# A linear-attention layer feeding a Mish expert: decaying three states with a diagonal matrix on TensorE, one step's row sums on VectorE, and a new order of instructions

## The chip, the cores and the metric

The kernel runs on one core of a Trainium2 chip. The metric is the device time of one execution in microseconds (us); the kernel before is given by the median of three runs, 466.11 us (465.73 to 466.19). The engines are TensorE (PE in the profile, with its weight loads as PEld), VectorE (DVE), ScalarE (ACT), GpSimd (POOL) and SyncE (SP), which issues most of the DMA transfers.

## The reference

Two stages, batch 4, 8 heads, 768 positions, head size 48; then 3072 tokens, model size 384, hidden size 2048, all float32.

```python
for t in range(S):                                   # recurrent attention, per head
    cur = einsum('bhd,bhe->bhde', u * k[t], v[t])
    y[t] = einsum('bhd,bhde->bhe', r[t], state + cur)
    state = w[:, :, None] * state + einsum('bhd,bhe->bhde', k[t], v[t])
x = y as (tokens, heads * head_dim)
h = x @ w_in
g = h * tanh(softplus(h))
return g @ w_out
```

## The kernel before

**Attention.** The positions are cut into chunks of 64. A "step" s is one of 24 pieces of work: one chunk of two of the four batches, all heads; four steps (one "group" of 512 tokens, 128 positions of every batch) make the input of one pass of the second stage. A step loads `rk` (r and k, transposed), `rkn` or `kn` (k, and r where needed, by position) and `v`. VectorE scales `rk` by powers of the decay (`scale`, L640). TensorE makes scores (`scores`, L725), which VectorE copies under a mask into a matrix `P` whose diagonal holds row sums of u times r times k (`attend`, L746; `diag`, L694). The row sums are made in one of three ways (`dots`, L648): steps below `N_SQ` with a TensorE product into `yt`, steps below `N_PE` with 16 one-column float32 products into `pa` (in `scores`), later steps with three VectorE operations on `rkn` (L686 to L691), which need r in the load and the table `un`. Then TensorE makes the outputs (`rows_y`, L799, for steps from 2; `spread_y`, L772, for steps 0 and 1) from the state carried so far and from `P`, and the products for the new state (`state_products`, L957). Two steps can be under way at once: each of the two sets of states is updated every second step (`update_state`, L932): VectorE multiplies the state by the decay over 64 positions and adds the products from two PSUM banks (L947, L952). The function has another branch, for steps in `decayed(s)`: there TensorE has added diag(decay) times the state to the same PSUM sums (`decays`, L837), and the state is only copied out. With `N_DEC = 2` no step takes it. A table for k, the "token table" (L345), is made with TensorE once, from the matrices `dw` that hold the decay on a diagonal.

**Second stage.** Six groups of 512 tokens, each with 16 tiles of hidden columns. An "up" tile is a product of x and the first weight matrix into one of two `hp` banks; it is evacuated to `hb` (L1312), goes through a sigmoid, an arctangent and a sine on ScalarE (L1094 to L1100) and products on VectorE (L1110 to L1118), and a "down" tile adds its product with the second matrix to three `acc` banks. Group 0 uses plain float32 products for most tiles; the others split each factor in a high and a low part and use three products. Weight blocks (`raw`, 768 KB each) are converted from an integer form on ScalarE and VectorE (`convert`, L492, the last operation at L514) and split (`split`, L519).

**Order.** Every engine's instructions are emitted by a planner (`Flow`, L134): a list scheduler with modelled durations. Each piece of work is a generator that yields events to wait for and costs on engines; among those that are ready the earliest goes, ties by rank, and `SHIFT`, `RANK`, `CONVERT`, `LAG` and the like move ranks. The order of the first loads is the list `FIRST`, of those behind it `REST`. `LO0` to `HI1` say over which part of a group's 16 up tiles the next group's four steps are spread (`place`, L1033). `AHEAD_LEAST` and `AHEAD_MOST` bound the distance between up and down tiles.

**Idle products.** At the start TensorE runs products of zeros into the bank `idle`: ten 512-column ones first, then some ahead of the first pieces of work (`warm`, L389), as the table `WARM` says; some wait for a load or a conversion. At `dots0` 14 short ones (16 columns) stand in addition, at `attend0` 28 short ones stand in place of two full ones.

Of the kernel before, what the change touches and what calls it, by code (L numbers as in the profile page):

```python
# [61 lines left out]
    return q // 2, 2 * (q % 2) + j  # L62


N_DEC = 2
N_SQ, N_PE = 2, 6
OWN = 3
CHECK_AT, CHECK_STEP = 44, 3
DIAG_ACT = (0, 1, 2, 5, 6, 10)
AHEAD = 4  # L70
UNITS = [(h, c) for h in range(2) for c in range(AHEAD)] + [(None, f) for f in range(WG * AHEAD, NF)]

# [5 lines left out]
def first_use(c):  # L78
# [1 line left out]


FIRST = (
    ("rk", 0), ("rk", 1), ("raw", 0), ("rkn", 3), ("v", 0), ("rkn", 1), ("rk", 2), ("rkn", 2), ("raw", 1), ("v", 1),
    ("rkn", 0), ("v", 3), ("v", 2), ("rk", 3),
)
REST = (
    ("raw", 2), ("raw", 3), ("un", 0), ("raw", 4), ("rk", 4), ("v", 4), ("raw", 5), ("raw", 6), ("rkn", 4), ("raw",
    8), ("raw", 7), ("raw", 9), ("raw", 10), ("raw", 14), ("raw", 11), ("raw", 12), ("raw", 13), ("raw", 15),
)
LAND0, LAND = 3.15, dict(rk=1.32, v=0.66, raw=1.96, rkn=0.5, un=0.78)  # L90
# [3 lines left out]
PAIRS = ()  # L94
BY_STEP = 0
FROM, FROM2 = 8, 14
X_SPLIT = 2
CONVERT = (1848.944, -4805.376, -1293.02, -2635.977)
LAG = 6
AHEAD_LEAST, AHEAD_MOST, DOWN = 3, 8, 0  # L100
LO0, HI0, LO1, HI1 = 0.0, 0.8, 0.05, 0.65
LAT, LAT0 = 0.15, 0.13
PE_GAP = 33
DVE_OWN = 0.02
COLD, COLD_END = 1.0, 0.0
WARM0, WARM_MIN, FILL = 10, 0.3, 0.28
WARM_END = 14.0
SHORT, LEFT_OUT = dict(dots0=14, attend0=28), ("attend0",)
WARM = dict(
    dots0=(("rk0", 2),), attend0=((None, 2),), dots1=((None, 1),), attend1=((None, 4),),  # L110
    outputs1=((None, 2), ("bent0", 3), ("whole0", 2), ("masked1", 4)),
# [2 lines left out]
BLOCK0, BLOCK, ASK, HELD, FETCH = 445, 256, 0.7, 2.9, 2.5  # L114
PATIENCE = dict(dve=0.1, act=0.1, pe=0.3)
URGENT = 8
RANK = dict(token_table=-1938.0, keys=833.2, first_state=-421.9)

COST = dict(dve=1.0)
FREE = dict(pe=5.6, act=2.8, dve=1.0, pool=1.7, sp=1.0, landed=1.0)  # L120
# [2 lines left out]


SHIFT = dict(
    attend10=98.0, attend5=51.0, convert11=-5.0, convert6=32.0, convert7=-243.0, convert9=122.0, diag10=-20.0,
    diag6=24.0, dots10=19.0, dots5=30.0, dots7=-71.0, dots8=121.0, evacuate10=-99.0, evacuate13=-164.0,
    evacuate22=-66.0, finish2=31.0, finish9=-62.0, gate10=141.0, gate12=-83.0, gate2=-42.0, gate3=54.0, gate8=-83.0,
    keys11=-152.0, keys5=24.0, mix0=-2.0, mix18=-54.0, mix5=-59.0, mix8=-31.0, mix9=-95.0, outputs9=-134.0,
    scale5=-174.0, split14=-67.0, split3=2.3, split4=73.0,  # L130
)


# [113 lines left out]
class Us(float):  # L247
    n = 0
# [17 lines left out]
def rwkv_mish_kernel(ctx, tc, rkT, rkN, vN, wT, w_in, w_out, consts, rkF, vF, wF, uF, outT):  # L266
    nc = tc.nc
# [9 lines left out]
    un = const.tile([128, DM], F32, name="un")  # L277
# [89 lines left out]
    def matmul(out, lhsT, rhs, **flags):  # L367
        nonlocal count
        ins = nc.tensor.matmul(out, lhsT=lhsT, rhs=rhs, **flags)  # L369
        first, count = count, count + (4 if lhsT.dtype == F32 else 2)  # L370
        k = (count - 1 - BLOCK0 % BLOCK) // BLOCK
        if k != (first - 1 - BLOCK0 % BLOCK) // BLOCK:
            crossed[k] = ins
        return ins
# [14 lines left out]
    def warm(name):  # L389

        z = zeros.bitcast(BF16)[:, :1]
        for after, n in WARM.get(name, ()):
            flow.begun += 2 * n
            for k in range(0 if name in LEFT_OUT else n):
                ins = matmul(idle, lhsT=z.broadcast_to([128, 128]), rhs=z.broadcast_to([128, 512]), start=True, stop=True)
                if after in marks and not k:
                    tc.add_manual_dep(ins.ins, marks[after].ins.name, sync, reason="no idle product goes too soon")
        for _ in range(SHORT.get(name, 0)):
            nc.tensor.matmul(
                idle[:32, :16], lhsT=z.broadcast_to([128, 32]), rhs=z.broadcast_to([128, 16]), start=True, stop=True  # L400
            )

    pa = ps.tile([128, 2, 512], F32, name="pa", tag="pa")
    for i in range(2):
# [5 lines left out]
    idle = ps.tile([128, 512], F32, name="idle", tag="acc0")  # L410
# [283 lines left out]
    def diag(s):  # L694
        yield f"sd{s}"
        if s >= 2:
            yield f"out{s - 2}"
        engine = yield {"act": 1.15} if s in DIAG_ACT else {"dve": 0.68}
        sd = sums.pop(s)
# [96 lines left out]
    def decayed(s):  # L796
        return 2 <= s < min(N_DEC, NS - 2)

# [82 lines left out]
    def outputs(s):  # L881
# [33 lines left out]
        if not rows:  # L915
            flow.start(first_state(s), s + RANK["first_state"], name=f"first_state{s}")
        elif not last:
# [548 lines left out]
    for s in range(NS):  # L1466
        if s < 2:
            flow.start(spread_v(s), rank(s) + 0.0045, 0.0, f"spread_v{s}")
        for k, thread in enumerate((load_step, load_v, scale, dots, diag, keys, attend, outputs)):
            if thread is keys and s >= NS - 2 or s <= B and thread in (load_step, load_v):  # L1470
                continue
            if thread is keys and s < B:
                flow.start(keys(s), s + (RANK["keys"] if s < 2 else -899.8), 0.0, f"keys{s}")
                continue
# [4 lines left out]
    for h in range(2) if FROM < WG * AHEAD else (None,):  # L1479
        flow.start(split_x(h), X_SPLIT, 0.0, f"split_x{'' if h is None else h}")  # L1480
    flow.start(load_rest(), -1200, 0.0)
    flow.start(prologue(), -1100, 0.0, "prologue")
    flow.start(token_table(), RANK["token_table"], 0.0, "token_table")
    for c in range(len(W_ORDER)):
        i, f = W_ORDER[c]
        at = first_use(f) + (LAG - L_OUT if i else -L_IN) + c / 1000
        flow.start(convert(c), CONVERT[c] if c < len(CONVERT) else at, 0.0, f"convert{c}")
    for n, (i, f) in enumerate(S_ORDER):
        first = first_use(f) if split_early((i, f)) else NF + f * WG
        flow.start(split(n), first + (LAG - L_OUT if i else -L_IN) + n / 1000, 0.0, f"split{n}")  # L1490
    flow.start(ups(), 1000, 0.0)
# [10 lines left out]
    with tc.If(in_range < 128 * N_FLAGS):  # L1502
# [3 lines left out]
        with tc.tile_pool(name="any1", bufs=1) as work:  # L1506
# [4 lines left out]
            z = work.tile([128, N, D], F32, name="z")  # L1511
# [39 lines left out]
        with tc.tile_pool(name="any2", bufs=1) as work:  # L1551
# [15 lines left out]
            z = zeros.bitcast(BF16)[:, :1]  # L1567
# [123 lines left out]
```

## Time and profile before

| | us |
|---|---|
| median of three runs | 466.11 |
| lowest, highest | 465.73, 466.19 |
| the profiled execution | 465.52 |
| its span, first to last instruction | 463.7 |
| TensorE busy | 454.9 (98%) |
| VectorE busy | 368.9 (80%) |
| ScalarE busy | 398.4 (86%) |
| mean granted TensorE clock | 0.990 |

Times within the profile count from the first instruction. Busy times are unions over an engine's instructions; a product that TensorE runs is drawn with its start and a modelled end, and products overlap, so the step from one start to the next tells more than a product's length. A float32 product is recorded as two.

### The profile page before, as it was taken

The numbers are of one execution on the slowest core, as the hardware profiler recorded it, in microseconds if no ns is written. First come the engines' busy times: TensorE is split into PE (matmuls) and PEld (weight loads), VectorE is DVE, ScalarE is ACT, GpSimd is POOL, SyncE is SP. The second block draws the span as 40 slices with busy tenths as digits, with TensorE's granted clock in tenths as the row PEclk, the third lists the DMA queues.
The fourth block names the chain that finished last, engine by engine and source line by source line (L and its number), as shares of the span: only waits on it lengthen the run. The fifth ranks groups of instructions, "written<-read, shape, count | busy, mean of one in ns | idle before, by whom it ended". The sixth has DMA issues, their size and how long they took to land.

```text
span 463.7 us, 11622 instructions
## 1 busy us (share of the span) xinstructions
PE 454.9 (98%) x4966; PEld 385.4 (83%) x4966; DVE 368.9 (80%) x584; ACT 398.4 (86%) x515; POOL 4.4 (1%) x31
## 2 busy tenths in 40 slices
PE   8999999999999999999999999999999999999995
PEld 5688988756887888888888888888888888888884
DVE  6899999999799995699956789974898746646752
ACT  5678989999899897787899888899888899999981
POOL 1000000000000000000000000000000000000000
PEclk8899999999999999999999999999999999999999
DMA  8866765730422230334241545432353222142001
GB/s 294 324 221 212 278 220 174 259 107 1 166 87 84 69 103 9 121 131 144 90 154 54 191 158 201 157 112 69 146 174 109 75 80 69 68 136 70 1 1 72
DMA packets 20169, 60.16 MB, mean 130 GB/s; under 512 B 3312, under 2 KB 4304, under 8 KB 20112
## 3 DMA queue, kind: packets, MB, share of 16 engines
q1 hardware_dynamic: 17664, 55.11, 34.9%
q10 hardware_dynamic: 2448, 4.25, 2.4%
q8 instruction: 40, 0.66, 0.6%
q14 instruction: 17, 0.14, 0.1%
HBM read 52.57 MB, written 4.72 MB: 124 GB/s over the span
## 4 chain that ended last, share of the span: by engine, by line
PE 74%; ACT 11%; DVE 10%; issue 2%; DMA 1%; ACTq 1%; SPq 0%; DVEq 0%
PE hp L369 33%; PE acc L369 32%; PE pa L369 4%; DVE hb L1110 2%; PE yt L369 2%; ACT fa L1100 2%; ACT L1094 2%; ACT fa L1094 2%; ACT fa L1097 2%; ACT L1100 1%; PE idle L369 1%; DVE gl L1118 1%; DMA rk<-in_rkT_dram 1%; DVE w L532 1%; ACT we L451 1%
## 5 line engine op out<-in xcount | busy, mean ns | idle before, releaser
L369 PE MATMUL hp<-x,w 128*128 128x512 f32 x720 | 169.0, 381 | 0.9 <-DVE hb L1312 0.9
L369 PE MATMUL acc<-gh,w 128*128 128x512 f32 x492 | 158.2, 381 | 0.0
L369 PEld LDWEIGHTS hp<-x,w 128*128 128x128 f32 x720 | 135.2, 189 | 20.8 <-DVE hb L1312 1.1
L369 PEld LDWEIGHTS acc<-gh,w 128*128 128x128 f32 x492 | 93.0, 189 | 13.5
L369 PE MATMUL acc<-gl,w 128*128 128x512 f32 x246 | 92.6, 379 | 0.0
L1110 DVE TENSOR_TENSOR hb<-hb,fa 128x1024 f32<-128x1024 f32 x40 | 48.9, 1221 | 36.8 <-ACT fa L1100 36.6
L1094 ACT ACT_TABLE_LOAD x47 | 60.3, 1283 | 5.7 <-DVE hb L1110 4.6
L1100 ACT ACT_TABLE_LOAD x47 | 60.3, 1283 | 1.7 <-DVE rkn L686 0.9
L1094 ACT ACTIVATE fa<-hb,small 128x1024 f32<-128x1024 f32 x48 | 55.2, 1151 | 2.1 <-DVE hb L1110 1.5
L369 PEld LDWEIGHTS acc<-gl,w 128*128 128x128 f32 x246 | 46.5, 189 | 6.6
L1097 ACT ACTIVATE fa<-fa 128x1024 f32<-128x1024 f32 x48 | 50.7, 1057 | 1.1 <-ACT fa L1094 0.3
L1312 DVE COPY hb<-hp 128x512 f32<-128x512 f32 x48 | 32.7, 685 | 23.2 <-PE hp L369 22.9
L1100 ACT ACTIVATE fa<-fa 128x1024 f32<-128x1024 f32 x47 | 49.7, 1058 | 0.5
L1118 DVE TENSOR_TENSOR gl<-hb,gh 128x1024 fp32r<-128x1024 f32 x40 | 48.8, 1219 | 1.0 <-ACT gh L1114 0.4
L1312 ACT COPY hb<-hp 128x512 f32<-128x512 f32 x48 | 28.0, 583 | 18.8 <-PE hp L369 18.7
L369 PE MATMUL acc<-gf,wraw 128*128 128x256 f32 (+1 forms) x132 | 37.8, 439 | 0.8 <-PE hp L369 0.8
L369 PEld LDWEIGHTS acc<-gf,wraw 128*128 128x128 f32 x132 | 25.8, 196 | 10.6 <-issue 7.0
L640 DVE TENSOR_TENSOR rk<-rk,TR 112x1024 f32<-112x1024 f32 x22 | 26.7, 1216 | 0.1
L1114 DVE CAST gh<-hb 128x1024 fp32r<-128x1024 f32 x32 | 22.0, 687 | 1.1
L369 PE MATMUL hp<-x,wraw 128*128 128x256 f32 x96 | 22.5, 386 | 0.0
L369 PEld LDWEIGHTS hp<-x,wraw 128*128 128x128 f32 x96 | 18.4, 196 | 2.0
L451 ACT ACTIVATE we<-wraw 128x768 f32<-128x768 f32 x16 | 19.3, 1207 | 0.7 <-ACT we L1152 0.4
(150 smaller groups left out, 554.6 us busy)
## 6 DMA issues: line engine op xcount, KB each, us to landing
wraw<-in_w_in_dram SPq DMA_DIRECT2D x16, 768.0 KB, 4.2
wraw<-in_w_out_dram SPq DMA_DIRECT2D x16, 768.0 KB, 4.9
rk<-in_rkT_dram SPq DMA_DIRECT2D x22, 512.0 KB, 4.4
rkn<-in_rkN_dram SPq DMA_DIRECT2D x18, 384.0 KB, 4.5
v<-in_vN_dram SPq DMA_DIRECT2D x22, 256.0 KB, 4.6
out_dram<-ob ACTq DMA_DIRECT2D x10, 256.0 KB, 2.1
x<-x SPq DMA_DIRECT2D x60, 32.0 KB, 2.0
out_dram<-we ACTq DMA_DIRECT2D x6, 256.0 KB, 2.2
```

The lines of the kernel that those rows point to most:

```text
L369: ins = nc.tensor.matmul(out, lhsT=lhsT, rhs=rhs, **flags)
L451: nc.scalar.activation(e, raw[:, :, 1].bitcast(F32), AF.Square, accum_out=to[:, 1:2])
L532: nc.vector.tensor_tensor(out=w[:, 1], in0=e, in1=w[:, 0].bitcast(F32), op=ALU.subtract)
L640: nc.vector.tensor_tensor(out=ab, in0=ab, in1=TR[:112].unsqueeze(1).broadcast_to([112, 4, NP, CK]), op=ALU.mult)
L1094: nc.scalar.activation(o.g, o.hb, AF.Sigmoid, bias=bias_ln2, scale=1.0)
L1097: nc.scalar.activation(o.g, o.g, AF.Arctan)
L1100: nc.scalar.activation(o.g, o.g, AF.Sin, scale=2.0)
L1110: nc.vector.tensor_tensor(out=o.hb, in0=o.hb, in1=o.g, op=ALU.mult)
L1114: (nc.scalar.copy if engine == "act" else nc.vector.tensor_copy)(out=o.gh, in_=o.hb)
L1118: nc.vector.tensor_tensor(out=o.gl, in0=o.hb, in1=o.gh.bitcast(F32), op=ALU.subtract)
L1312: (nc.scalar.copy if engine == "act" else nc.vector.tensor_copy)(out=to, in_=h)
```

## The change

States of steps 2 to 4 take the other branch: 16 products with the diagonal matrix on TensorE, accumulated with the state products, and two copies from PSUM, in place of one product and two additions on VectorE. Step 5's row sums move from TensorE to the three VectorE operations, so its load holds r as well (384 KB in place of 200). Diagonals of steps 3 and 7 move from VectorE to ScalarE, those of 0 and 10 from ScalarE to VectorE. The short idle products are gone, with the two full ones at `attend0` back in their place. The order of loads and the planner's ranks are new: v of step 0, fifth in `FIRST`, comes eighth; the steps of the second group are spread over 15% to 75% of the tiles of the first (before 0% to 80%), those of later groups over 0% to 90% (before 5% to 65%).

```diff
-N_DEC = 2
-N_SQ, N_PE = 2, 6
+N_DEC = 5
+N_SQ, N_PE = 2, 5
...
-DIAG_ACT = (0, 1, 2, 5, 6, 10)
+DIAG_ACT = (1, 2, 3, 5, 6, 7)
...
 FIRST = (
-    ("rk", 0), ("rk", 1), ("raw", 0), ("rkn", 3), ("v", 0), ("rkn", 1), ("rk", 2), ("rkn", 2), ("raw", 1), ("v", 1),
-    ("rkn", 0), ("v", 3), ("v", 2), ("rk", 3),
+    ("rk", 0), ("rk", 1), ("rkn", 3), ("raw", 0), ("rk", 2), ("rkn", 1), ("raw", 1), ("v", 0), ("rkn", 2), ("v", 1),
+    ("v", 2), ("rkn", 0), ("v", 3), ("rk", 3),
 )
 REST = (
-    ("raw", 2), ("raw", 3), ("un", 0), ("raw", 4), ("rk", 4), ("v", 4), ("raw", 5), ("raw", 6), ("rkn", 4), ("raw",
+    ("raw", 2), ("un", 0), ("raw", 3), ("raw", 4), ("rk", 4), ("raw", 5), ("rkn", 4), ("v", 4), ("raw", 6), ("raw",
...
-X_SPLIT = 2
-CONVERT = (1848.944, -4805.376, -1293.02, -2635.977)
-LAG = 6
-AHEAD_LEAST, AHEAD_MOST, DOWN = 3, 8, 0
-LO0, HI0, LO1, HI1 = 0.0, 0.8, 0.05, 0.65
+X_SPLIT = 5
+CONVERT = (2717.144, -4617.276, -1404.32, -2171.877)
+LAG = 4
+AHEAD_LEAST, AHEAD_MOST, DOWN = 1, 8, 0
+LO0, HI0, LO1, HI1 = 0.15, 0.75, 0.0, 0.9
...
-SHORT, LEFT_OUT = dict(dots0=14, attend0=28), ("attend0",)
...
-RANK = dict(token_table=-1938.0, keys=833.2, first_state=-421.9)
+RANK = dict(token_table=-1723.3, keys=662.4, first_state=-707.4)
...
 SHIFT = dict(
...
 )
...
-            for k in range(0 if name in LEFT_OUT else n):
+            for k in range(n):
...
-        for _ in range(SHORT.get(name, 0)):
-            nc.tensor.matmul(
-                idle[:32, :16], lhsT=z.broadcast_to([128, 32]), rhs=z.broadcast_to([128, 16]), start=True, stop=True
-            )
```

The 34 entries of `SHIFT` are replaced by 25 others.

## Rows read from the trace of the kernel before

**Rows 1.** The page: busy us of each engine, share, instructions.

```profile
PE 454.9 (98%) x4966; PEld 385.4 (83%) x4966; DVE 368.9 (80%) x584; ACT 398.4 (86%) x515; POOL 4.4 (1%) x31
```

**Rows 2.** Windows: stretch, its length, busy us by engine, clock, DMA share, GB/s.

```profile
9.40:13.10 3.70, 3.70 (x17) 2.29 (x13) 3.31 (x6) 2.89 (x12) 0.00 (x0) 0.50 1.04 418
13.10:15.00 1.90, 1.90 (x81) 1.80 (x80) 0.81 (x3) 0.66 (x3) 0.00 (x0) 0.65 1.02 376
20.10:37.00 16.90, 16.13 (x372) 13.62 (x368) 15.61 (x28) 12.30 (x27) 0.33 (x2) 1.00 0.60 201
37.00:140.00 103.00, 102.95 (x1238) 83.96 (x1239) 97.84 (x150) 96.92 (x127) 0.58 (x7) 1.00 0.49 168
140.00:285.00 145.00, 143.47 (x1730) 124.69 (x1729) 120.44 (x191) 125.07 (x156) 0.80 (x9) 1.00 0.32 107
285.00:445.00 160.00, 159.94 (x1244) 139.16 (x1244) 113.27 (x180) 145.72 (x163) 0.44 (x5) 1.00 0.31 104
445.00:463.70 18.70, 13.95 (x65) 11.89 (x63) 7.11 (x9) 7.05 (x9) 0.00 (x0) 0.94 0.13 46
```

**Rows 3.** Chain of waits, 70 to 90 us: start, us, what.

```profile
78.94 2.59 PE acc L369 x12
81.53 1.94 PE hp L369 x9
```

**Rows 4.** Chain of waits, 4 to 38 us.

```profile
6.15 0.44 PE idle L399 x14
...
7.57 0.83 PE idle L399 x28
...
11.51 1.73 PE idle L369 x4
...
15.10 2.51 PE idle L369 x11
...
19.40 0.81 PE pb L369 x16
...
36.24 0.81 issue
```

**Rows 5.** Instructions on the tile S, 20 to 60 us: duration ns min/median/max.

```profile
L977 ACT COPY S<-pb x4: 322/328/342, 23.6 to 25.1; 112x192 f32<-112x192 f32 x4
L947 DVE TENSOR_TENSOR S<-S,small x3: 550/551/555, 30.0 to 51.1; 112x384 f32<-112x384 f32 x3
L952 DVE TENSOR_TENSOR S<-S,hp x3: 343/348/353, 30.7 to 51.8; 112x192 f32<-112x192 f32 x3
```

**Rows 6.** Timeline of TensorE, 22.9 to 24.3 us: start, us, what.

```profile
22.94 0.58 PE L369 MATMUL pb<-v,kn 64*48 64x48 f32 x32
23.34 0.61 PE L369 MATMUL pa<-cst,q 48*64 48x1 f32 x32
23.79 0.67 PE L369 MATMUL pa<-first 48*64 48x64 f32 x32
```

**Rows 7.** Timeline of VectorE, 33 to 38 us.

```profile
34.13 0.55 DVE L947 TENSOR_TENSOR S<-S,small 112x384 f32<-112x384 f32 x1
...
35.99 0.95 DVE L514 CUSTOM_DVE_ANT_0 wraw<-wraw,we 128x1536 uint16<-128x1536 uint16 x1
```

**Rows 8.** Groups by line and shape: busy us, mean ns of one.

```profile
L707 DVE TENSOR_TENSOR P<-cst,sd 128x512 f32<-128x512 bf16 x18 | 12.3, 686 | 1.0 <-ACT sd L680 0.7
...
L644 DVE TENSOR_TENSOR q<-rk 112x512 f32<-112x512 f32 x4 | 2.7, 685 | 1.0 <-DMA rk<-in_rkT_dram 1.0
```

**Rows 9.** DMA issues: count, KB each, median us to landing.

```profile
wraw<-in_w_in_dram SPq DMA_DIRECT2D x16, 768.0 KB, 4.2
...
rk<-in_rkT_dram SPq DMA_DIRECT2D x22, 512.0 KB, 4.4
...
kn<-in_rkN_dram SPq DMA_DIRECT2D x4, 192.0 KB, 7.2
```

**Rows 10.** Timeline of all engines, 0 to 21 us.

```profile
10.18 0.21 DVE L876 COPY pre<-v 128x96 f32<-128x96 f32 x1 [0.39 <-DMA v<-in_vN_dram]
...
14.07 0.31 PE L369 MATMUL yt<-P,v 64*64 64x64 f32 x1
```

More of the change, by code (lines that the diff above doesn't have):

```diff
@@ L125 @@
 SHIFT = dict(
[L126 to L130, printed above, removed]
+    attend11=-26.0, attend8=-30.0, convert13=3.0, convert14=-47.0, convert6=112.0, convert9=292.0, diag7=63.0,
+    dots10=81.0, dots12=-5.0, dots9=-3.0, evacuate11=14.0, evacuate5=6.0, finish10=-36.0, gate11=-7.0, keys7=178.0,
+    keys8=36.0, mix3=83.0, outputs11=6.0, outputs12=-25.0, outputs3=-81.0, outputs6=-12.0, split1=63.0, split10=2.0,
+    split2=29.0, split3=27.0,
 )
```

## Prediction

> **What bounds the kernel.** I read the page first: TensorE is busy for 454.9 of 463.7 us, VectorE for 80%, ScalarE for 86% [rows 1]. Busy time of a pipelined engine can hide waits, so I went on to the windows, stretch by stretch. TensorE is idle for 0.77 us between 20.1 and 37, 0.05 between 37 and 140, 1.53 between 140 and 285, 0.06 from there to 445 [rows 2]: 2.4 us in 425. Then I checked that "busy" is real work. In the chain of waits 12 down products take 2.59 us and 9 up products 1.94 us [rows 3], 0.216 us each in both, although the one comes just after the other on the same engine and VectorE is full in that stretch. The products run at one pace with nothing hidden between them. From about 20 us on the end is set by how many products TensorE has to run and by these few stalls.
>
> The front differs. The chain runs on TensorE there too, but through idle products: 14 short ones (0.44 us), 28 short ones (0.83), 4 full ones (1.73) and 11 full ones (2.51) [rows 4]. The 4 take 0.43 us each and the 11 take 0.23 us each: the granted clock is 0.50 (1.2 GHz) from 9.40 to 13.10 and 0.65 on average to 15.00, before it is back at 2.4 GHz [rows 2]. The last 18.7 us are down products and the writing of the result; TensorE is idle there only for the final 4.75 us [rows 2].
>
> So the question for each edit is: how much does it add to or take from TensorE's stream, and does it make that stream wait?
>
> **Part 1, states that decay on TensorE.** For steps 2, 3 and 4 VectorE drops one product of the state with the decay (0.55 us) and two additions (0.35 us each), 1.25 us a step, 3.75 us in all [rows 5]. Two plain copies a step take their place, on whichever of ScalarE and VectorE the planner finds free; the nearest copy of this shape took 0.33 us on ScalarE [rows 5]. TensorE gains 16 float32 products a step, recorded as 32, because every such product counts as two. The trace has none of them. The state products, 32 records of the same 48 columns, took 0.40 us from their start at 22.94 to the next group at 23.34 [rows 6], but they use four tiles of the array in turn; the decays use only two (rows 0 to 47 to columns 0 to 47, and rows 64 to 111 to columns 64 to 111). The nearest rows with two tiles are the token table's, 16 records of 96 columns in 0.81 us [rows 4], 0.10 us a pair. Bounds: 0.40 us a step if the decays overlap as four; 16 pairs of the token table, 1.6 us, if columns don't matter. Scaled by columns (half), 16 pairs come to 0.8 us. I take 0.7, since the token table's figure holds the end of its group as well: **+2.1 us**, bounds +1.2 and +4.8, the latter unlikely, as it would make 48 columns as dear as 96.
>
> The token table's row bears on a rule of the Trainium skill ("TensorE: Matmul & The Clock Gate", Measured speedup vs the span model): a pack of tiles takes the time of one product plus some 4 ns for each further tile. By it a pack of two costs nearly what a pack of four does, and the estimate from that page and the state products would be 0.8 us a step, 2.4 us in all; with overlap as four the sum would hold 1.2. No run so far shows these products.
>
> What VectorE's relief is worth: the 0.77 us before 37 us are one wait, 0.81 us long in the chain, ahead of the first down products at 37.05 [rows 4]. They need the second matrix's first block, whose last conversion on VectorE runs from 35.99 to 36.94, behind the updates of the states of steps 2 and 3 [rows 7]. With 1.25 us of step 2's and 0.9 of step 3's update gone from ahead of it, this wait goes: **-0.8 us**, bounds -0.8 and 0 (if the new order puts other VectorE work there). Elsewhere the relief meets no wait in a stretch with 0.05 us of them, and gives nothing.
>
> **Part 2, sums of step 5 on VectorE.** TensorE drops 32 records of one column; the like group takes 0.45 us, from 23.34 to 23.79 [rows 6]: **-0.45 us**. VectorE drops a product of 0.69 us [rows 8] and gains two products and a sum over 384 columns, 0.55 us each by the state's product over as many columns [rows 5], so +0.95 us. It is busy for 97.8 of 103 us there, but TensorE waits for 0.05 [rows 2], so I cost it at nothing; the cover is that steps of the second group run ahead of their use, and without it the cost is 0.95 us. The load of step 5's rows grows where the DMA share is 0.49 [rows 2]: nothing. The sums now wait for that load, and queued behind them on VectorE are evacuations of up products; only a load later than the planner thinks would reach TensorE that way.
>
> **Part 3, diagonals.** Steps 3 and 7 leave VectorE for ScalarE, 0 and 10 go the other way, 0.69 us each on VectorE [rows 8]. Step 0's goes in between the scaling of step 1 and the first masked copy, and ScalarE is freed at that time: nothing.
>
> **Part 4, the front.** Dropping the short products takes 0.44 + 0.83 = 1.27 us out of the chain; two full idle products come back, 0.46 us at the full and 0.86 at the low clock by the rows of the 11 and of the 4 [rows 4]. If nothing waited, the front would gain 0.4 to 0.8 us. But the order of loads changes too: v of step 0 moves behind rk 2, a block of kn and a weight block, 512 + 192 + 768 KB [rows 9]. At the 376 to 418 GB/s of this stretch [rows 2] that is 3.6 to 4.0 us. VectorE's small copy that waits for v of step 0 began at 10.18 us [rows 10]; it would begin at 13.8 to 14.2 and take 0.2, and with the hand-over the output products of step 0 can start at 14.1 to 14.6. They start at 14.07 now [rows 10], between the 4 and the 11 idle products. So TensorE arrives earlier by half a microsecond and then waits for v: no gain, and a loss of 0 to 0.5. I take **+0.3 us**, bounds -0.8 (other products fill the wait) and +0.5.
>
> **Part 5, the order.** New ranks and paces spread the steps of groups 2 to 5 over 90% of a group's up tiles in place of 60%. That could clear the 1.53 us of stalls between 140 and 285, and could make new ones as long. I take 0, bounds -1.5 and +1.5. Downs may follow ups more closely; the tiles of down products that now stand after the last up tile cover the last gates, and nothing forces fewer: nothing.
>
> **Sum.** 2.1 - 0.8 - 0.45 + 0.3 = +1.15 us. The profiled execution took 465.52 us (a span of 463.7 and 1.8 around it) and would take 466.7; it lies 0.6 below the median of the runs shown, 466.11, so the median becomes **467.3 us**. About 0.2%, 0.9 us, is what this kernel's measurement can tell from no change.
>
> **Rivals.**
> *The wait for v is filled.* If the scores of step 2 are ready when TensorE comes free near 13.5 us, the front gains 0.8 instead of losing 0.3: +0.05 in the sum, 466.2 us. For it: rk 2 lands earlier. Against it: these scores wait for two VectorE operations that come after the conversion of the first block.
>
> *The low clock lasts longer.* In the rows the clock is back by 15.00 us, after a stretch in which TensorE ran without a break [rows 2]. If it now stands and waits for v in that stretch, and the clock stays at 1.2 GHz through the 11 idle products, they take 0.43 instead of 0.23 us each: +2.2 us on the sum, 469.5. For it: the wait would lie just ahead of the rise. Against it: it is well under a microsecond. The Trainium skill ("TensorE: Matmul & The Clock Gate", What's actually happening) says that the throttled state is the default and activity releases it, which favours this rival; the trace agrees so far as its rise comes after unbroken work.
>
> *VectorE sets the pace after all.* If the stretch up to 140 us is paced by VectorE, TensorE's extra products are hidden and the relief counts: 3.75 - 0.95 + 0.69 (steps 3 and 7 out, 10 back in) = 3.5 us, less the 0.3 of the front: 462.9. It decides for faster once 1.2 us of the relief arrives. For it: VectorE is busy for 97.8 of 103 us [rows 2]. Against it: products at 0.216 us each without gaps.
>
> **Chances.** Forecast 0.47 (slower 0.40, same 0.07); v's wait filled 0.23 (same 0.17, slower 0.03, faster 0.03); low clock 0.13 (slower); VectorE 0.17 (faster 0.14, same 0.03). Faster 0.17, same 0.27, slower 0.56. The forecast's own range, with decays at 0.5 to 0.8 us a step, the first wait gone or not and the front at 0 to 0.5, is 466.4 to 468.7. The range that holds 8 in 10 reaches toward VectorE's case as far as half of its relief with the later stalls left, 464.8, and past the low clock's case to the dearest decays, 470.0.
>
> **What would show it.** Decays: 32 records a step between 27 and 55 us, 0.7 us a group, and no multiplication of the state on VectorE before step 5. The wait ahead of the first down products gone. The copy of v of step 0 near 14 us, and TensorE idle just before the first outputs. The clock back at the same time as now. TensorE's idle time from 140 to 285 us near 1.5 us. I am wrong if decays cost 0.4 us a step, if the first outputs start before 14 us, or if the later stalls differ by more than a microsecond.

## The result: slower by 1.1%, and the profile after

The changed kernel takes 471.56 us (median of four, 469.96 to 471.89) against 465.92 for the kernel before, measured beside it (465.57 to 466.19): a ratio of 1.0113, interval 1.0092 to 1.0133. The forecast was 467.3 us, range 464.8 to 470.0: the sign came out, the size did not. The profiled execution took 471.35 us with a span of 469.6, against a span of 463.7: +5.9 us to explain.

In the changed kernel's listing the same code stands two to six lines earlier (the matrix product is L367 for L369, the evacuation L1306 for L1312). The page, and the windows in the columns of [rows 2]:

```profile
PE 457.1 (97%) x4990; PEld 385.0 (82%) x4990; DVE 373.1 (79%) x593; ACT 393.8 (84%) x504; POOL 4.8 (1%) x31
```

```profile
9.40:13.10 3.70, 1.29 (x36) 0.66 (x33) 3.52 (x7) 2.85 (x10) 0.00 (x0) 0.97 1.04 406
12.85:19.68 6.83, 5.82 (x59) 2.89 (x59) 5.81 (x8) 1.87 (x5) 0.00 (x0) 0.50 0.95 363
20.10:37.00 16.90, 16.90 (x548) 15.02 (x544) 11.96 (x21) 13.56 (x34) 0.18 (x2) 1.00 0.58 192
37.00:140.00 103.00, 99.65 (x1205) 79.76 (x1201) 95.10 (x146) 91.51 (x125) 0.58 (x7) 1.00 0.48 161
140.00:285.00 145.00, 144.74 (x1653) 125.79 (x1643) 120.74 (x191) 125.98 (x152) 1.27 (x8) 1.00 0.33 111
```

Two stretches are worse. Between 9.40 and 13.10 TensorE is busy for 1.29 of 3.70 us, where it was busy throughout [rows 2]. Between 37 and 140 it idles for 3.35 us in place of 0.05. One stretch is better: 0.26 us idle from 140 to 285, in place of 1.53. The clock is the other news: full from 9.40 to 12.85, half from 12.85 to 19.68. Before, its half-speed stretch lay earlier and ended before the outputs of step 1:

```profile
7.59:14.41 6.82, 6.82 (x120) 5.20 (x122) 5.32 (x8) 5.28 (x19) 0.00 (x0) 0.50 1.02 395
```

The chain of waits after (start, us, what) shows what the front now hangs on:

```profile
4.58 9.14 DMA v<-in_vN_dram
13.72 0.14 issue
13.86 0.34 PE yt L367
...
15.42 4.60 PE idle L367 x11
...
22.62 2.80 PE hp L367 x12
```

and the first up products in the same view of the kernel before:

```profile
20.21 2.80 PE hp L369 x12
```

The up products start 2.41 us later. TensorE's timeline after, with the idle time before an instruction in brackets:

```profile
9.04 1.03 PE L367 MATMUL idle<-zeros 128*128 128x512 bf16 x4
10.00 0.69 PE L367 MATMUL pb<-rk 48*64 48x64 f32 x32
13.86 0.34 PE L367 MATMUL yt<-P,v 64*64 64x64 f32 x1 [3.17 <-DMA v<-in_vN_dram]
...
30.21 0.20 PE L367 MATMUL yt<-S,pre 48*48 48x48 f32 x1
...
30.55 0.20 PE L367 MATMUL hp<-S,pre 48*48 48x48 f32 x1
...
31.25 0.20 PE L367 MATMUL hp<-S,pre 48*48 48x48 f32 x1
...
31.58 0.20 PE L367 MATMUL yt<-S,pre 48*48 48x48 f32 x1
...
39.08 0.81 PE L367 MATMUL hp<-x,wraw 128*128 128x256 f32 x3
40.00 0.46 PE L367 MATMUL acc<-gf,wraw 128*128 128x256 f32 x1
...
53.09 0.49 PE L367 MATMUL hp<-x,wraw 128*128 128x256 f32 x1 [0.27 <-DVE x L1010]
...
102.10 0.70 PE L367 MATMUL acc<-gf,wraw 128*128 128x512 f32 x1 [1.75 <-DVE gf L1102]
```

From this the 5.9 us divide by place. Up to the first up product: +2.41. From there to the first down product (40.00 after; 36.24 + 0.81 = 37.05 before [rows 4]): 2.95 - 2.41 = +0.54, of which the wait ahead of it, 0.81 before and 39.08 + 0.81 to 40.00 = 0.11 after, is -0.70, so that the decays of steps 2 and 3 come to 1.24, 0.62 us each (TensorE runs the same products there in both traces, but for the decays). Behind the first down product: 5.9 - 2.95 = +2.95; less 0.62 for step 4, taken like the other two, and plus the predicted 0.45 for step 5's sums, new waits make some +2.8.

### The profile page after: what moved, and what is told of

It is laid out like the page before. It is cut to its first block, busy times and chain, and to the rows that moved or that the text cites. A ratio compares the mean times of both kernels' runs of the same rounds, so it can differ in the third digit from the quotient of the medians.

```text
span 469.6 us, 11665 instructions
## 1 busy us (share of the span) xinstructions
PE 457.1 (97%) x4990; PEld 385.0 (82%) x4990; DVE 373.1 (79%) x593; ACT 393.8 (84%) x504; POOL 4.8 (1%) x31
## 4 chain that ended last, share of the span: by engine, by line
PE 73%; ACT 10%; DVE 7%; DMA 5%; SPq 2%; issue 1%; ACTq 0%
PE hp L367 34%; PE acc L367 33%; PE pa L367 3%; DMA wraw<-in_w_out_dram 2%; PE yt L367 2%; DMA v<-in_vN_dram 2%; ACT L1094 2%; ACT fa L1094 1%; DMA wraw<-in_w_in_dram 1%; ACT fa L1091 1%; ACT L1088 1%; DVE w L526 1%; ACT wraw L498 1%; ACT w L524 1%; ACT fa L1088 1%
## 5 line engine op out<-in xcount | busy, mean ns | idle before, releaser
L367 PE MATMUL hp<-x,w 128*128 128x512 f32 x720 | 169.7, 382 | 0.2 <-DVE hb L1306 0.2
L367 PE MATMUL acc<-gh,w 128*128 128x512 f32 x492 | 157.8, 380 | 0.0
L367 PEld LDWEIGHTS hp<-x,w 128*128 128x128 f32 x720 | 134.9, 189 | 20.7 <-issue 0.9
L367 PEld LDWEIGHTS acc<-gh,w 128*128 128x128 f32 x492 | 93.0, 189 | 13.5
L367 PE MATMUL acc<-gl,w 128*128 128x512 f32 x246 | 92.7, 379 | 0.0
L1306 DVE COPY hb<-hp 128x512 f32<-128x512 f32 x57 | 39.0, 686 | 23.8 <-PE hp L367 23.6
L367 PEld LDWEIGHTS acc<-gl,w 128*128 128x128 f32 x246 | 46.5, 189 | 6.6
L367 PE MATMUL acc<-gf,wraw 128*128 128x256 f32 (+1 forms) x132 | 38.7, 441 | 2.5 <-DVE gf L1102 1.8
L1306 ACT COPY hb<-hp 128x512 f32<-128x512 f32 x39 | 22.7, 582 | 17.7 <-PE hp L367 16.6
L367 PEld LDWEIGHTS acc<-gf,wraw 128*128 128x128 f32 x132 | 25.5, 196 | 12.2 <-issue 6.0
L367 PE MATMUL hp<-x,wraw 128*128 128x256 f32 x96 | 22.8, 387 | 0.7 <-ACT hb L1306 0.4
L447 DVE TENSOR_REDUCE small<-we 128x1 f32<-128x768 f32 x16 | 15.2, 949 | 8.9 <-ACT we L445 8.9
L367 PEld LDWEIGHTS hp<-x,wraw 128*128 128x128 f32 x96 | 18.3, 196 | 3.1 <-DVE x L1010 0.7
```

The lines of the kernel that those rows point to most:

```text
L447: v.tensor_reduce(out=to[:, 0:1], in_=e, axis=AX.X, op=ALU.min)
L1306: (nc.scalar.copy if engine == "act" else nc.vector.tensor_copy)(out=to, in_=h)
```

## Experiments

Each ratio is to the kernel before on the same chip, with a 95% interval. Single executions of one kernel differ by more here than in the runs first shown: the kernel before ranged from 464.6 to 470.7 us in the widest series. So verdicts rest on medians, and a profile is one execution. The record also has each execution's mean granted clock, and part of the spread goes with it.

### The load of v of step 0

**Loaded fifth again in the changed kernel.** The small copy goes to GpSimd, so that no other engine's order changes.

```diff
-        for what, s in FIRST:
+        for what, s in FIRST[:4] + FIRST[7:8] + FIRST[4:7] + FIRST[8:]:
...
-        (nc.scalar.copy if engine == "act" else nc.vector.tensor_copy)(
+        (nc.gpsimd.tensor_copy if s == 0 else nc.scalar.copy if engine == "act" else nc.vector.tensor_copy)(
```

> The changed kernel (471.56 us), with v of step 0 loaded fifth again and its small copy moved from ScalarE, where it stands behind a weight conversion, to GpSimd; every other order is kept. Theory of the late load: the changed kernel's TensorE waits 3.2 us for v of step 0 just before the first outputs and then runs 11 idle products in 4.6 us instead of 2.5; without the wait the first up product, at 22.6 us, comes 2 to 4 us earlier and the time falls to 467.5 to 469.6 us. Rival, that later waits for weight blocks take the gain back: the front moves but the time stays above 470.6 us. Rival, that v's place does not matter: no change of the front, 471.6 us.

Measured: 468.50 us, ratio 1.0065 (1.0041 to 1.0089), 3.1 us below the changed kernel. Windows and TensorE's timeline of it:

```profile
9.40:13.10 3.70, 3.54 (x91) 2.13 (x92) 3.52 (x6) 2.98 (x10) 0.60 (x1) 1.00 1.02 409
13.10:15.00 1.90, 1.36 (x13) 0.47 (x15) 1.90 (x4) 1.16 (x3) 0.00 (x0) 1.00 1.06 392
```

```profile
10.85 0.22 PE L367 MATMUL yt<-P,v 64*64 64x64 f32 x1
...
18.13 0.92 PE L367 MATMUL hp<-x,wraw 128*128 128x256 f32 x3
```

The wait is gone, the clock stays at full speed through the front, the outputs of step 0 start at 10.85 in place of 13.86 us, and the up products at 18.13 in place of 22.55 (22.62 in the chain above). This profile is the fastest of twelve executions. Seven of them were granted a mean clock of 0.998 or more, with a median of 468.33 us; the other five, at 0.991 to 0.996, took 469.24 to 472.00. With v late, in the changed kernel and in the run of the seventh block below, none of 16 executions was granted more than 0.996.

**Loaded ninth in the kernel before**, again with the copy on GpSimd; nothing else is changed.

```diff
-        for what, s in FIRST:
+        for what, s in FIRST[:4] + FIRST[5:9] + FIRST[4:5] + FIRST[9:]:
```

> The kernel before with v of step 0 loaded ninth, behind kn, rk 2 and the second weight block, and its small copy on GpSimd; every other order kept. Theory that the late load costs the front by itself: TensorE waits for v until about 14.3 us; if it arrives at 13.5 (low clock in the front) the loss is 0.3 to 0.8 us, if it arrives at 10.5 (full clock) the 11 idle products run at 1.2 GHz too and the loss is 2 to 3 us; median 466.5 to 468.5 us. Rival, that the front of the changed kernel is slow for the clock alone and the load does not matter: 465.6 to 466.3 us.

Measured: 470.82 us, ratio 1.0100 (1.0076 to 1.0124): +4.6 us against 466.26 beside it, more than either expectation. TensorE's timeline, and the window of the half-speed clock:

```profile
15.23 0.34 PE L369 MATMUL yt<-P,v 64*64 64x64 f32 x1 [1.78 <-DMA v<-in_vN_dram]
...
23.15 0.92 PE L369 MATMUL hp<-x,wraw 128*128 128x256 f32 x3
```

```profile
8.99:19.23 10.24, 8.46 (x99) 5.26 (x98) 7.79 (x11) 5.37 (x18) 0.81 (x1) 0.50 0.97 378
```

In this profile (468.75 us, the fastest of six) the up products start 3.0 us later than in the kernel before (20.14 in this view), behind a wait of 1.78 us and with the clock at half speed for 10.24 us. Here the clock was low before the wait began, as it was in the kernel before, but it came back at 19.23 in place of 14.41 us. Behind the start of the up products the span is 443.7 us, against 443.6 before: nearly all of this profile's loss lies in the front. The late load alone costs most of what the change cost; v stands one place later here than in the changed kernel and lands at 15.10 us, not 13.72.

**The changed kernel without its 11 idle products.** It leaves out work whose results nothing reads.

```diff
-            for k in range(n):
+            for k in range(0 if name == "outputs1" else n):
```

> The changed kernel without the 11 idle products ahead of the outputs of step 1; they take 4.6 us there. Theory that these products, at the low clock, stand in the chain: the outputs of step 1 start near 16 us instead of 19.95, the first up product near 18.5 instead of 22.6, time 467.5 to 469.0 us. Rival, that they bring the clock back: the low clock lasts past 24 us, up products take 5.2 us a tile pair instead of 2.6, and the time is 470.5 us or more.

Measured: 473.31 us, ratio 1.0155 (1.0135 to 1.0175). Windows and timeline:

```profile
14.82:25.06 10.24, 7.38 (x134) 6.54 (x135) 6.54 (x9) 4.72 (x16) 0.00 (x0) 0.50 0.68 251
```

```profile
16.25 0.95 PE L367 MATMUL pa<-cst,q 48*64 48x1 f32 x26
19.94 0.28 PE L367 MATMUL pa<-cst,q 48*64 48x1 f32 x3 [2.73 <-issue]
```

The rival came out, in time and clock. The idle products are not what holds the front: without them TensorE stood 2.73 us, waiting for nothing that the profile shows, and the clock was low until 25.06 us. A stand of this kind comes in other runs too, as here in TensorE's timeline of the kernel with both repairs (below):

```profile
16.23 0.45 PE L367 MATMUL pa<-cst,q 48*64 48x1 f32 x17 [0.82 <-issue]
```

It splits the same group of 32 one-column products: after 15 of them where the 11 idle products stand ahead, after 26 where they are left out. It moved by as many products as were dropped, so it keeps to a place in TensorE's stream.

**The kernel before without short idle products**, two full ones in their place.

```diff
-SHORT, LEFT_OUT = dict(dots0=14, attend0=28), ("attend0",)
+SHORT, LEFT_OUT = dict(), ()
```

> The kernel before with the 42 short idle products left out and the two full ones at attend0 back; the rest as it was. By the prediction's sum the front gains 0.4 to 0.8 us when nothing waits: 465.2 to 465.6 us. Rival, that the chain then waits for data anyway: 465.7 to 466.2 us. Rival, that the short products held up the clock: the low clock lasts longer and the time rises by 1 us or more, above 467 us.

Measured: 465.61 us, ratio 0.9992 (0.9970 to 1.0014). This part of the change costs and gives nothing that can be told. It raises the clock: all twelve executions were granted 0.994 to 0.998, and 27 of the 35 of the kernel before beside them less than 0.994. In its profile the outputs of step 0 start at 12.32 us in place of 14.07, but TensorE then stands 1.81 us in the group of one-column products, after 15 of them, and the up products start no earlier (20.32 us).

### The seventh weight block

After 37 us the changed kernel has a second wait for a transfer. The timeline of SyncE's queue, after and then before:

```profile
38.23 4.25 SPq L1020 DMA_DIRECT2D x<-x  x6
42.57 1.25 SPq L598 DMA_DIRECT2D rkn<-in_rkN_dram  x1
43.87 0.43 SPq L602 DMA_DIRECT2D v<-in_vN_dram  x1
44.35 0.43 SPq L482 DMA_DIRECT2D wraw<-in_w_out_dram  x1
...
50.61 0.33 SPq L482 DMA_DIRECT2D wraw<-in_w_out_dram  x1
```

```profile
34.28 3.76 SPq L1026 DMA_DIRECT2D x<-x  x6
38.14 0.52 SPq L488 DMA_DIRECT2D wraw<-in_w_out_dram  x1
...
42.94 0.42 SPq L488 DMA_DIRECT2D wraw<-in_w_out_dram  x1
```

One weight block is under way at a time, so the issue of the next shows when one has landed. The block issued at 38.14 before is issued at 44.35 after, behind six copies of x and two loads on the same queue; its successor goes at 50.61 in place of 42.94. The six copies stood ahead of it before, too. New are the two loads, and that the copies go 3.95 us later, as the products that make x do (2.41 us at the first up products, 1.24 by the decays). Where v came early, in the first run above, the copies went at 34.84 and the block at 40.13 us.

**That block issued ahead of the copies of x**, in the changed kernel. This does not restore the order of before but goes beyond it.

```diff
         yield {"sp": 3.6}
+        if s == 3:
+            early_block()
         for k in range(KT):
...
```

> The changed kernel with one transfer moved: the seventh weight block is issued ahead of the six small copies of x of steps 2 and 3 on SyncE's queue, not behind them and two loads of steps. Theory of the late block: it is issued near 37 us (when the block before it has landed) instead of 44.35, every later block comes some 4 to 7 us earlier, TensorE's idle time between 37 and 140 us falls from 3.35 us to under 1.2, and the time falls to 469.0 to 469.9 us. Rival, that these stalls come from VectorE's and ScalarE's work in the new order: idle time above 2.7 us, time 471 to 472 us.

Measured: 469.47 us, ratio 1.0072 (1.0048 to 1.0097), 2.1 us below the changed kernel. What TensorE waited for between 37 and 140 us (engine, line, waited for: us, times, longest):

```profile
PE acc L367 <- DVE gf L1118: 1.9, 1, 1.9
PE acc L367 <- DVE wraw L508: 0.6, 1, 0.6
```

The waits for x and hb, 0.3 and 0.4 us in the changed kernel, are gone. The longest one stayed, 1.9 us for gf near 100 us, so both expectations were half right. This profile (471.76 us) is the slowest of twelve: behind that wait, which ended at 100.70 us, the clock was at 0.50 once more, from 101.08 to 104.49. So it does not show where the 2.1 us of the median were saved. The wait comes from VectorE, here in the timeline of the changed kernel:

```profile
98.17 0.94 DVE L508 CUSTOM_DVE_ANT_0 wraw<-wraw,we 128x1536 uint16<-128x1536 uint16 x1
...
99.50 0.95 DVE L508 CUSTOM_DVE_ANT_0 wraw<-wraw,we 128x1536 uint16<-128x1536 uint16 x1
...
100.83 1.22 DVE L1102 TENSOR_TENSOR gf<-hb,fa 128x1024 f32<-128x1024 f32 x1
```

The gate's product gf stands behind the conversions of two weight blocks, and behind parts of a state's update and a copy that the cuts leave out.

**Both repairs together.**

> The changed kernel with both repairs, v of step 0 loaded fifth and the seventh weight block issued ahead of the copies of x. Theory (both costs are real and only partly the same): 3.1 us from the load and about half of the block's 2.1 us, since the stall at 52 us was already gone with the load repaired; 467.0 to 468.0 us, and what is left over the kernel before is the decays (+1.9), the sums (-0.45) and the stall near 96 us. Rival (each repair only moved the waits for instructions and the clock about): no better than the load alone, 468.5 us or more.

Measured: 466.78 us, ratio 1.0021 (1.0005 to 1.0038): 4.8 of the 5.6 us are back. The sum of the two single gains would be 5.2. The profiled execution, at the median, has the clock at full speed throughout the front, as the kernel before had not. Its first down product starts at 36.67 us, 0.4 before that of the kernel before; behind it the span is 1.6 us longer than before (464.9 - 36.67 against 463.7 - 37.05), in place of 2.95 in the changed kernel.

### The order as a whole

**The kernel before with the new load order, ranks and paces**, and **the changed kernel with the old ones**; the planner lays out each anew. `FIRST`, `REST`, `X_SPLIT`, `CONVERT`, `RANK` and `SHIFT` go along with the lines shown; the second edit is the reverse of the first.

```diff
-LAG = 6
-AHEAD_LEAST, AHEAD_MOST, DOWN = 3, 8, 0
-LO0, HI0, LO1, HI1 = 0.0, 0.8, 0.05, 0.65
+LAG = 4
+AHEAD_LEAST, AHEAD_MOST, DOWN = 1, 8, 0
+LO0, HI0, LO1, HI1 = 0.15, 0.75, 0.0, 0.9
...
```

> The work of the kernel before (no decays on TensorE, step 5's sums on TensorE, short idle products, old diagonals) with the load order, paces, ranks and shifts of the changed kernel, planned again. Theory that the order carries most of the loss (front 2.4 us, stalls 2): 469.0 to 471.0 us. Rival, that the decays on TensorE carry it: 465.5 to 467.5 us. The plan is made for other work, so a loss of its own of 1 us more would not be a surprise.

> The work of the changed kernel (decays, step 5's sums on VectorE, new diagonals, no short idle products) with the load order, paces, ranks and shifts of the kernel before, planned again. Theory that the order carries most of the loss: decays +1.9, sums -0.45 and no more than 1 us of waits for instructions, 466.5 to 468.4 us. Rival, that the work carries it, as the kernel before with decays alone suggests (469.6 us): above 469 us.

Measured: 483.50 us, ratio 1.0371 (1.0349 to 1.0392), and 482.70 us, ratio 1.0336 (1.0306 to 1.0366). The first misses both expectations by 12 us and more. The second lies above 469 us, as its rival had it, but by 13.7 us, far more than the decays cost in any run. In the first one wait for gf lasted 6.0 us; in the second there are seven waits of 1.2 us and more, spread over the run. The constants fit the work that they go with and not the other, so an exchange of them tells nothing about their share in the change.

### The decays

**The decays alone, in the order of before.** The planner keeps its costs for the old work, so each instruction stands where it stood; 96 records are added for the three steps and copies replace the updates.

```diff
-        if decayed(s):
+        if 2 <= s < 5:
             decays(1)
...
-            nc.vector.tensor_tensor(out=S[:, b], in0=S[:, b], in1=new[b][r112], op=ALU.add)
+            if 2 <= s < 5:
+                nc.vector.tensor_copy(out=S[:, b], in_=new[b][r112])
+            else:
+                nc.vector.tensor_tensor(out=S[:, b], in0=S[:, b], in1=new[b][r112], op=ALU.add)
```

> The kernel before with the decays of steps 2 to 4 alone, in its own order: 96 more product records on TensorE, and on VectorE two copies a step in the places of the additions, no multiplication. By the prediction's sum 2.1 us more on TensorE and 0.8 less of the wait before the first down products: 467.2 us (466.7 to 467.6). Rival, that the decays overlap as four tiles: 466.3 us. Rival, that VectorE sets the pace up to 140 us: under 465.2 us.

Measured: 469.62 us, ratio 1.0079 (1.0055 to 1.0103), 2.4 us above the expectation. Its chain of waits has two pieces that the kernel before has not:

```profile
29.00 1.01 issue
...
35.10 0.93 issue
```

Both stalls lie in the middle of a group of state products, with nothing waited for. Counted in TensorE's records, products and weight loads together, they stand exactly 256 apart. The page's list of queues has 40 transfers of instructions on one queue, 0.66 MB together, 16 KB each. The Trainium skill ("Trainium Architecture — The Big Picture", The software stack) gives an instruction 64 bytes; an estimate by that figure is 256 instructions in 16 KB, as far apart as the stalls.

**The same with two full idle products for the 42 short ones**, 80 records fewer ahead of that place.

> The kernel before with the decays of steps 2 to 4 on TensorE, and two full idle products in place of the 42 short ones, so 80 records fewer stand ahead of the state products. Theory (the stalls of 1.19 and 1.11 us in the run of the decays alone are waits for the next block of 256 instructions): they leave the products at which they stood, and any stall of that kind stands again a whole number of 256 records away, some 80 records later in the work; time 467.5 to 469.5 us. Rival (the decays themselves hold the state products up, by the bank they share): stalls of over 1 us at the same products, in the middle of the state products of steps 2 and 3, and a time of 469.6 us as with the decays alone.

Measured: 469.08 us, ratio 1.0071 (1.0051 to 1.0090). The stalls at 29 and 35 us are gone, so the decays do not hold the state products up. One of the kind stands in TensorE's timeline later, in step 4's decays:

```profile
52.59 0.20 PE L369 MATMUL hp<-S,pre 48*48 48x48 f32 x1 [1.25 <-issue]
```

Counted from the start, it is 504 records behind the later of the two, twice 256 to within the few that a trace can miss. An instruction transfer of that queue lay ahead of it, from 50.28 to 51.21 us.

**The states back on VectorE in the kernel with both repairs**: of all three steps, of step 4, of steps 2 and 3 (shown; `decay` stands for the table of the decay over 64 positions). The order stays.

```diff
-        if decayed(s):
+        if decayed(s) and s not in (2, 3):
             decays(1)
...
-                (nc.scalar.copy if engine == "act" else nc.vector.tensor_copy)(out=S[:, b], in_=new[b][r112])
+                if s not in (2, 3):
+                    (nc.scalar.copy if engine == "act" else nc.vector.tensor_copy)(out=S[:, b], in_=new[b][r112])
+                else:
+                    if not b:
+                        nc.vector.tensor_tensor(out=S, in0=S, in1=decay, op=ALU.mult)
+                    nc.vector.tensor_tensor(out=S[:, b], in0=S[:, b], in1=new[b][r112], op=ALU.add)
```

> The changed kernel with both repairs, and the states of steps 2 to 4 updated on VectorE again, each instruction in its place of the changed order: the 96 records of the decays are left out of TensorE's stream, and 3 multiplications and 6 additions stand where the 6 copies stood, on VectorE. Theory (the decays cost what their records take, 0.62 us a step, and VectorE's relief buys nothing): 1.9 us below the kernel with both repairs, 465.2 to 466.2 us, level with the kernel before. Rival (the new order needs VectorE's relief): stalls ahead of the down products grow by what VectorE gets back, and the time is level with the kernel with both repairs or above it.

> The changed kernel with both repairs, and the state of step 4 alone updated on VectorE again; steps 2 and 3 decay on TensorE. Theory (VectorE's relief is used ahead of the first down products, 28 to 41 us, and not later): 0.6 us below the kernel with both repairs, 466.0 to 466.5 us. Rival (step 4's update on VectorE is what made TensorE wait at 49.7 us for x, because it stands ahead of the copies of x and of a conversion): a stall of 1.0 to 1.5 us near 49 us, and a time of 467.2 to 468.0 us.

> The changed kernel with both repairs, and the states of steps 2 and 3 updated on VectorE again; step 4 decays on TensorE. Theory (relief used ahead of the first down products): the stall ahead of them stays at 1.5 to 2 us, and 1.2 us of dropped products are used up by it: 466.8 to 468.0 us. Rival (that stall was a weight block that happened to land late in that one run, and only step 4's relief counts): 1.2 us below the kernel with both repairs, 465.3 to 466.0 us, which would beat the kernel before.

Measured: 468.98 us, ratio 1.0066 (1.0047 to 1.0085), for all three; 467.97 us, 1.0041 (1.0023 to 1.0060), for step 4; 468.43 us, 1.0045 (1.0026 to 1.0065), for steps 2 and 3. The first theory fails: without the decays this order is slower, not faster, by 2.2 us against both repairs in the same series. For the single steps the intervals overlap with that of both repairs. The granted clock sorts this: of the executions at 0.997 and more the medians are 466.58 us with both repairs (8 executions), 466.71 with steps 2 and 3 on VectorE (5), 467.62 with step 4 (9) and 469.02 with all three (5). So at the same clock, as far as these few tell, steps 2 and 3 change nothing, and step 4 costs 1.0.

Steps 2 and 3: TensorE's and VectorE's timelines, first with both repairs (decays in), then with the two steps on VectorE.

```profile
36.67 0.46 PE L367 MATMUL acc<-gf,wraw 128*128 128x256 f32 x1
```

```profile
33.82 0.36 DVE L945 COPY S<-hp 112x192 f32<-112x192 f32 x1 [1.04 <-PE yt L367]
...
35.35 1.22 DVE L1118 TENSOR_TENSOR gf<-hb,fa 128x1024 f32<-128x1024 f32 x1
```

```profile
34.22 0.81 PE L367 MATMUL hp<-x,wraw 128*128 128x256 f32 x3
36.64 0.46 PE L367 MATMUL acc<-gf,wraw 128*128 128x256 f32 x1 [1.61 <-issue]
```

```profile
33.13 0.55 DVE L949 TENSOR_TENSOR S<-S,small 112x384 f32<-112x384 f32 x1
...
35.32 1.22 DVE L1125 TENSOR_TENSOR gf<-hb,fa 128x1024 f32<-128x1024 f32 x1
```

The first down product starts at 36.67 and at 36.64 us. It needs gf, gf stands on VectorE behind step 3's update, and it runs at 35.3 us either way. With 1.24 us less work TensorE stands 1.61 us (the profile names no releaser, but gf ends 0.1 us before the product starts); with the decays it is VectorE that stands, 1.04 us ahead of step 3's copy. Both spans are 464.9 us. The stall came out as the theory for this run had it, the time 0.4 us above its range. Step 4, in TensorE's timeline of the run that takes this step alone back:

```profile
50.15 1.35 PE L367 MATMUL hp<-x,wraw 128*128 128x256 f32 x5 [1.26 <-DVE x L1031]
```

Copies of x stand behind step 4's update on VectorE, and a wait of 1.26 us takes the place of 0.62 us of products, as the rival for this run had it.

None of these versions beats the kernel before.

## Why the prediction was wrong

**What bounds the kernel.** TensorE's stream does, but "elsewhere the relief meets no wait" does not follow from waits of 0.05 us. In the new order the first down product follows gf on VectorE, with or without the decays, and VectorE would make TensorE wait near 50 us if step 4's update stood there. An order laid out so that nothing waits shows no wait where relief is needed.

**Part 1, decays: near in size.** The two groups of 16 records in the timeline above take some 0.35 us each from start to start, partly over the next group; the net by the sum of places is 0.62 us a step, 1.9 us in all if step 4 is like the others, for a forecast of 0.7 and 2.1. The estimate from the Trainium skill's pack rule ("TensorE: Matmul & The Clock Gate", Measured speedup vs the span model) was 0.8 us a step: the measured 0.62 lies below it. The wait ahead of the first down products shrank by 0.70 for a forecast of 0.8. In the order of before the same decays cost 2.8 us (469.08 against 466.24 beside it) to 3.7 us (0.79%), with waits for instructions that I had no row for.

**Part 2 and Part 3**: no wait between 37 and 140 us in the profile after names the sums or the diagonals; the sums' 0.45 us was not measured by itself.

**Part 4, the front: the step that failed.** The time of v was nearly right: it landed at 13.72 us and the outputs of step 0 start at 13.86, 0.2 us earlier than before [rows 10] and than the 14.1 to 14.6 of the forecast, which had outputs before 14 us as a sign of being wrong. Wrong was that TensorE "comes free near 13.5 us". I took 0.4 to 0.8 us off its old arrival, at the old clock. But without the short products, which alone raises the clock in the kernel before, the 4 idle products and the scores ran at full clock, 10.00 - 9.04 = 0.96 us for the 4 in place of 1.73 [rows 4], and TensorE was done at 10.7 and stood for 3.17 us. In this wait, at 12.85 us, the clock fell. The outputs took 15.42 - 13.86 = 1.56 us in place of 15.10 - 14.07 = 1.03, and the 11 idle products 4.60 in place of 2.51: -0.21 + 0.53 + 2.09 = +2.41, the whole of the front's loss, for a forecast of +0.3. Against the kernel before, which ran its front at the low clock, the wait adds nothing by its own length, and the clock behind it makes the loss. That is the rival "the low clock lasts longer", priced at +2.2 and given 0.13 because the wait would be "well under a microsecond". Against the changed kernel with v fifth, at full clock, wait and clock both count: 3.0 us to the outputs of step 0, 4.4 to the up products. The Trainium skill ("TensorE: Matmul & The Clock Gate", What's actually happening) has the throttled state as the default and activity as what releases it; the trace agrees, with 0.50 from 12.85 to 19.68 us, from the long wait on, and 1.00 from 9.40 to 15.00 where v came early. Over all profiles it is much the same: with v late the low clock of the front ended at 19.2 to 25.1 us (five profiles); with v early it ended by 15.0 or never came (eight), but for two, at 20.9 and 24.0 us, in which TensorE had stood for 1.2 to 1.8 us shortly before. Undone and done alone, the load bears it out: 3.1 us back in the changed kernel, 4.6 us lost in the kernel before.

**Part 5, the order: mis-sized.** I gave it 0, with bounds of 1.5 us either way, and it made some +2.8, of which the windows draw 2.0 as idle time (a wait begins before the modelled end of the product ahead of it). The 1.53 us between 140 and 285 went, as the prediction thought possible, though by more than the microsecond that it named as a sign of being wrong; 3.35 us came between 37 and 140. Part of it is the seventh weight block behind six copies of x and two loads on SyncE's queue: 2.1 us by issuing it ahead of them, which is more than the change had moved, since the copies stood ahead of it before and only went earlier. I had counted what stands ahead of v in the first loads, and not what stands ahead of a block in the later ones. The wait for gf near 100 us, behind two blocks' conversions on VectorE, is part of the rest; no run took it away, though it is 0.9 us with both repairs.

**The sum.** 1.9 - 0.7 - 0.45 + 2.4 + 2.8 = 5.95 us, for 5.9 in the span; the last term was found as what the others leave. With both repairs 0.2% remain, but not because the order is mended: 1.6 us behind the first down product are made up in part by a front at full clock. The prediction's own range, added up again, ends at 468.6, not 468.7, which changes nothing.

**What stays open.** With steps 2 and 3 on VectorE the profiled execution takes as long as with the decays, 464.9 us of span, and yet the median of its runs is 1.65 us higher (range 466.55 to 471.19). As far as so few executions tell, the granted clock accounts for it: 7 of its 12 executions were below 0.997, with a median of 468.65 us, and 3 of the 11 with both repairs, with 468.80. Why more of them ran at the lower clock is not shown, the two series having run on different chips. Nor was it tried why a wait for instructions comes in one order and not in another, beyond moving it. The kernel's planner has such a wait as a modelled term (`BLOCK = 256`), and the runs of the decays in the old order kept its plan for fewer products; whether a new plan would avoid the waits was not run.

## What to carry to other kernels

Where a load is moved behind others at the start, work out when the engine that needs it arrives, at either clock; if it would stand, price the work behind the wait at the low clock as well. A transfer's place counts on the queue that issues it: list what stands ahead of it there, small copies too, and when that can go. Where the medians of two variants differ, see whether their executions were granted the same clock, and whether the change itself moved it. A stretch without waits tells what the present order does, not what relief would be worth in another order; taking the relief away again, in the new order, measures it.

## What the runs showed of the hardware

TensorE can stand for 0.4 to 2.7 us with nothing waited for, in the middle of a group. Where two such stalls came in one run they lay 256 records apart, and 80 records fewer ahead of them moved them to other work; in the front the stall kept to one place in TensorE's stream in five profiles (0.44, 0.82, 1.14, 1.81 and 2.73 us). Each of these eight ended 1.3 to 1.5 us after a transfer on the instruction queue had ended: 18.55 and 19.94 us in the run without the 11 idle products, 28.68 and 30.01, 34.50 and 36.03 in that of the decays alone, 51.21 and 52.59 in the one after it. That queue had 39 transfers in the three runs with 9788 to 9850 records on TensorE and 40 in those with 9914 to 10122. This speaks for waits for the next block of TensorE's instructions; what makes a block late is not shown. A load that fills the DMA engines is not needed: they were busy for 0.09 of the transfer that ended at 28.68 us, and it took 0.97 us like others. If so, many small products can cost more than their time, since each record of a product comes with one of a weight load; this was not measured by itself.
